# Denominators and gating logits of three pairs in one bank, normalized behind the transposes

## The chip, the cores and the metric

The kernel runs on one core of one Trainium2 chip. The metric is the device time of one execution in microseconds (us). A core has TensorE (PE in the profile, its weight loads PEld), VectorE (DVE), ScalarE (ACT), GpSimd (POOL) and SyncE (SP); each takes its instructions in a fixed order and waits for others by semaphores. PE writes its results into PSUM, in banks of 512 fp32 columns by 128 partitions. SP and POOL also start DMA transfers, each from a queue of its own.

## What is computed

Attention with a soft cap on the scores, over 8 batches, 12 heads, 448 tokens and a head size of 64, followed by a mixture of experts with one expert out of 8 per token:

```python
scores = cap * np.tanh(scale * np.matmul(q, k.transpose(0, 1, 3, 2)) / cap)
attn = np.exp(scores - np.max(scores, axis=-1, keepdims=True))
attn = attn / (np.sum(attn, axis=-1, keepdims=True) + 1e-09)
x = np.matmul(attn, v)                     # -> (3584, 768), a token's 12 heads side by side
logits = x @ w_gate + modality_bias[modality_id]
e_idx = np.argmax(logits, axis=1)
# gate_w: the softmax of the logits at e_idx
out[mask] = gate_w[mask, None] * (np.maximum(x[mask] @ w1[e], 0.0) @ w2[e])   # mask = e_idx == e
```

## The kernel before

**Attention.** The work goes by pairs of heads: 6 pairs a batch, 48 in all, numbered g. For a pair, `kq` holds keys and queries of both heads (head j in the 64 partitions from 64 j). `prep(g + 1)` loads the next pair: `kq` and `va` (the values) by SP, `hi` (a rounded copy of `kq`, which POOL's queue loads with a conversion) and `lo`, the remainder, on DVE (line 432). `scores` has four steps: three of 128 own keys of each head, and one in which the last 64 keys of both heads share the 128 partitions. Each step makes products hi x hi, lo x hi, hi x lo on PE (line 443), then tanh and exp on ACT (lines 445, 446) into `pt`, transposed: keys on partitions, queries along the columns. Two score tiles are in PSUM in turn.

The weighted values of pair g − 1 are made during pair g: `weigh_own` between the second and third score step, `weigh_shared` behind the fourth; `xT` has the two heads' dimensions on the partitions and queries along columns. `add_up` sums `pt` over the key blocks on DVE into `tot`. A pair later (g − 2 during pair g) `normalize` multiplies `tot` by a matrix of ones on PE, which gives the denominators `den` already spread over the 64 partitions of their head; DVE takes the reciprocal of this 128 x 448 tile (line 463) and multiplies (line 465, `xn`). `rows_out` transposes `xn` to rows of tokens (line 482, four transposes), and DVE copies them into `xs` (line 484). Behind every third pair `gate` makes the gating logits of the three pairs, in three groups of 32 columns of one bank `glog` (line 491), summed over the two triples of a batch, and POOL starts the store of `xs` to `xd` in DRAM.

**Routing.** Behind a batch's last pair `logits` transposes `glog` to tokens (lines 498 to 502), and `route` finds on DVE the expert of each token, its weight, and by two small matmuls (`rank`, lines 232 and 233) its place among that expert's tokens; an iota (line 247) and four indirect DMAs (line 256) on POOL write token number and weight into the map `mapd`. After seven batches `early_slot` chooses the expert of a first slot of 384 tokens, whose map (`rows`), tokens (`gather`, by indirect DMA on POOL) and first-layer weights (`load_raw`, `split_w`) are fetched while the last pairs run; `MOVES` puts the transposes of the gathered tokens. After the last batch `slots` plans all other slots on DVE.

**Experts.** Per slot `ffn1` (8 blocks of 128 columns, 18 matmuls each) and `ffn2` (six half-outputs of 24 matmuls); `ahead` fetches the next slot's map rows and tokens, which `ffn2` transposes between its half-outputs.

**Order.** What passes through `pin` keeps the program's order on its engine; this is so for nearly all of PE's attention work and for SP's loads. All other instructions are ordered engine by engine when the kernel is built, by a planner that takes what is ready first by its own estimate of times. So the order on DVE, ACT and POOL is fixed before the run, and an instruction that waits holds all that stand behind it on its engine.

## Time and profile before

| | |
|---|---|
| median of 3 runs | 1071.52 us (1067.74 to 1072.17) |
| profiled execution | 1074.64 us, span 1073.1 us |
| busy: PE / DVE / ACT / POOL | 935.8 / 693.0 / 566.2 / 148.8 us |
| mean granted TensorE clock | 0.938 |
| first expert matmul | 543.0 us from the start of the span |

The profile gives the busy time of each engine, the groups of instructions with their mean duration in ns, what an engine waited for in the idle time before an instruction (in square brackets or behind "<-", with the line of the releasing instruction), and in a stretch of time the TensorE clock that the throttle granted, as a share of full speed. A busy PE is not PE at its peak, since matmuls are pipelined; differences between the starts of instructions that follow without a pause say what a block of them costs.

### The profile page before, as it was taken

Reading aid. Unit: us, or ns where it says so; the run is one execution under the profiler, and the core shown is the slowest. Engines: PE = TensorE matmul, PEld = TensorE weight load, DVE = VectorE, ACT = ScalarE, POOL = GpSimd, SP = SyncE. Lnnn points to the kernel's source line nnn. Section 1 sums busy time; section 2 is a strip of 40 time slices with the busy share of each in tenths; the row PEclk is TensorE's granted clock in tenths of the full one; section 3 lists DMA queues with packets and bytes.
Section 4 is the critical chain, followed back from the end, with each engine's and each line's share of the span. In section 5 each row is a group of like instructions: output and inputs, shape, how many; then the busy total and the mean of one; then the engine's idle time right before and its main releaser. Section 6 shows DMA issues by size and latency. Waiting matters only on the chain. (4 is left out here: it accounts for less than half of the span.)

```text
span 1073.1 us, 14468 instructions
## 1 busy us (share of the span) xinstructions
PE 935.8 (87%) x5232; PEld 713.9 (67%) x5232; DVE 693.0 (65%) x978; ACT 566.2 (53%) x759; POOL 148.8 (14%) x191
## 2 busy tenths in 40 slices
PE   7786878689787786874789999999999999999996
PEld 3343444344343443432359999999999999998896
DVE  5897888969798787884975443434444444447762
ACT  7675667667575675654614444434443434345551
POOL 2002020010202002021013202020201011101100
PEclk9898889989898898887889999999999999999997
DMA  5454435525354354446417646453636463535760
GB/s 152 140 159 134 141 120 162 166 79 166 119 166 138 94 165 124 146 121 164 146 37 237 217 131 211 150 193 132 206 118 206 133 191 133 177 135 197 246 202 10
DMA packets 53803, 162.62 MB, mean 152 GB/s; under 512 B 9422, under 2 KB 9934, under 8 KB 53712
## 3 DMA queue, kind: packets, MB, share of 16 engines
q1 hardware_dynamic: 38000, 105.78, 31.1%
q0 software_dynamic: 15568, 55.72, 16.6%
q8 instruction: 46, 0.75, 0.3%
q14 instruction: 45, 0.37, 0.1%
q10 hardware_dynamic: 144, 0.00, 0.0%
HBM read 139.96 MB, written 22.69 MB: 152 GB/s over the span
## 5 line engine op out<-in xcount | busy, mean ns | idle before, releaser
L445 ACT ACTIVATE th<-sc,isc 128x896 f32<-128x896 f32 x192 | 169.5, 909 | 139.6 <-PE sc L443 135.2
L446 ACT ACTIVATE pt<-th,cabs 128x896 f32<-128x896 f32 x192 | 176.8, 949 | 2.9
L689 PE MATMUL ph<-x,al 128*128 128x384 f32 (+2 forms) x528 | 168.0, 318 | 0.0
L711 PE MATMUL py<-bh,hh 128*128 128x384 f32 x464 | 158.4, 342 | 2.7 <-ACT bh L641 2.7
L463 DVE RECIPROCAL rec<-den 128x448 f32<-128x448 f32 x48 | 141.7, 2953 | 27.0 <-PE den L461 26.5
L711 PE MATMUL py<-bh,hl 128*128 128x384 f32 x464 | 155.7, 336 | 0.0
L711 PE MATMUL py<-bl,hh 128*128 128x384 f32 x464 | 155.2, 334 | 0.0
L685 PE MATMUL ph<-x,ah 128*128 128x384 f32 x384 | 129.3, 337 | 1.6 <-DVE plan L383 1.5
L686 PE MATMUL ph<-x,ah 128*128 128x384 f32 x384 | 129.3, 337 | 0.0
L642 DVE TENSOR_TENSOR bl<-raw,bh 128x768 fp32r<-128x768 f32 x88 | 82.1, 955 | 68.3 <-ACT bh L641 62.3
L472 PE MATMUL xT<-pt,va 128*64 128x448 f32 x576 | 121.0, 556 | 0.0
L641 ACT CAST bh<-raw 128x768 fp32r<-128x768 f32 x88 | 71.7, 840 | 70.4 <-DMA raw<-in_w_dram 60.1
L689 PEld LDWEIGHTS ph<-x,al 128*128 128x128 f32 x528 | 102.1, 193 | 0.7 <-issue 0.7
L642 DVE TENSOR_TENSOR al<-raw,ah 128x1024 fp32r<-128x1024 f32 x66 | 79.6, 1223 | 31.6 <-ACT ah L641 31.2
L472 PEld LDWEIGHTS xT<-pt,va 128*64 128x64 f32 x576 | 43.8, 147 | 78.2 <-issue 71.2
L443 PE MATMUL sc<-hi 64*128 64x448 f32 (+1 forms) x336 | 93.2, 484 | 2.9 <-ACT th L445 2.3
L482 PE MATMUL tp<-ident,xn 128*112 128x128 f32 x192 | 31.2, 287 | 73.4 <-DVE xn L465 68.2
L482 PEld LDWEIGHTS tp<-ident,xn 128*112 128x112 f32 x192 | 21.0, 138 | 102.7 <-issue 77.9
L711 PEld LDWEIGHTS py<-bh,hh 128*128 128x128 f32 x464 | 87.0, 188 | 3.1 <-ACT bh L641 3.0
L721 POOL DMA_INDIRECT out_dram<-ot,mt x29 | 33.1, 1141 | 396.3 <-ACT ot L716 319.5
L711 PEld LDWEIGHTS py<-bh,hl 128*128 128x128 f32 x464 | 87.1, 188 | 0.2 <-DVE hl L696 0.2
L711 PEld LDWEIGHTS py<-bl,hh 128*128 128x128 f32 x464 | 87.2, 188 | 0.0
(155 smaller groups left out, 1424.2 us busy)
## 6 DMA issues: line engine op xcount, KB each, us to landing
raw<-in_w_dram SPq DMA_DIRECT2D x66, 512.0 KB, 4.4
raw<-in_w_dram SPq DMA_DIRECT2D x88, 384.0 KB, 4.0
kq<-in_kq_dram SPq DMA_DIRECT2D x47, 480.0 KB, 3.4
hi<-in_kq_dram POOLq DMA_DIRECT2D x46, 480.0 KB, 6.9
va<-in_v_dram SPq DMA_DIRECT2D x48, 256.0 KB, 4.1
xd<-xs POOLq DMA_DIRECT2D x16, 672.0 KB, 4.4
mapd<-pay,pos POOLq DMA_INDIRECT x32, 3.3
xg<-xd,mt POOLq DMA_INDIRECT x30, 6.0
```

The source lines that it names most:

```text
L443: pin(pe.matmul(sc[:, j, :S], k[rows, ks], q[rows, KC2:], start=i == 0, stop=i == 2))
L445: nc.scalar.activation(th[:, :n], sc[:, :n, :S], AF.Tanh, scale=self.isc)
L446: nc.scalar.activation(pt[:, 2 * step : 2 * step + n], th[:, :n], AF.Exp, scale=self.cabs)
L463: nc.vector.reciprocal(rec, den[:, :S])
L472: pin(pe.matmul(xT[j * D : (j + 1) * D, :S], va[:, u * D : (u + 1) * D], pt[:, u], start=i == 0, stop=False))
L482: pin(pe.transpose(tp[:CP, c * 128 : (c + 1) * 128], xn[:, c * CP : (c + 1) * CP], self.ident))
L641: a = self.nc.scalar.copy(hi, raw)
L642: b = self.nc.vector.tensor_tensor(lo, raw, hi, op=ALU.subtract)
L685: nc.tensor.matmul(ph[:, :w], hi[:, fs], self.x[:, k, 0, :w], start=first, stop=False)
L686: nc.tensor.matmul(ph[:, :w], hi[:, fs], self.x[:, k, 1, :w], start=False, stop=False)
L689: nc.tensor.matmul(ph[:, :w], lo[:, fs], self.x[:, k, 0, :w], start=False, stop=last)
L711: nc.tensor.matmul(py[:, :HALF], self.h[a][:, f, rows], self.w2s[f][c][:, cs], start=i == 0, stop=i == 3 * FC - 1,)
```

## The change

- The denominators are no longer spread over 64 partitions. `sums` collects for three pairs at a time, in one bank with 32 columns per pair, four parts: the column sums of `tot` of head 0 and of head 1, those of the shared keys `sh`, each by a weight matrix `pick` with ones in column 16 or 17, and the gating logits of both heads from the values that aren't normalized (columns 0 to 15). They stand behind `weigh_own`: parts 0 and 1 in the second pair of the next triple, parts 2 and 3 in its third.
- `by_token` transposes this bank for each triple; `logits` takes the reciprocals of 24 columns per partition and multiplies the logits. `rows_out` transposes the `xT` that isn't normalized, copied from PSUM to SBUF pairs before, and multiplies by the reciprocals as it leaves PSUM. The three pairs of a triple are transposed together, one pair behind the logits.
- The exp of the shared keys goes to a tile `sh` of its own; `add_up`'s two half adds go.
- `route` is cut in two: the part up to the counts behind the logits, `rank` and the writing of the map behind the next pair's `weigh_own`; both `rank` matmuls and the count are pinned. For the last batch the second part stands behind the second block of the first `ffn1`, and `slots` behind the fourth; the fetch for the next slot then comes behind this `ffn1`.
- The early slot's map is read one pair later, its gather two pairs later; four first-layer weight blocks are loaded at once behind pair 45, with four staging buffers instead of three.
- One PSUM bank for `xT` instead of two, one more for the transposes.

```diff
-NU = 2 * KU + 1
 OWN = KU * 128
 KC2 = OWN + 2 * KR
 QK = KC2 + S
+GE = 2 * E
...
+        self.pick = cpool.tile([128, 3, GW], F32, name="pick")
+        nc.vector.memset(self.pick, 0.0)
+        for j in range(2):
+            nc.vector.memset(self.pick[:, j, GE + j : GE + j + 1], 1.0)
+            nc.vector.memset(self.pick[j * KR : (j + 1) * KR, 2, GE + j : GE + j + 1], 1.0)
...
         nc.vector.tensor_tensor(self.acc, before[:, C - 1], oh[:, C - 1], op=ALU.add)
+        yield
         rank = ps.tile([128, 512], F32, name="rank", tag="small")
         rk = rank[:CP, : C * E]
-        nc.tensor.matmul(rk, self.tri, oh.rearrange("p c e -> p (c e)"), start=True, stop=False)
-        nc.tensor.matmul(rk, self.ones[:, :CP], before.rearrange("p c e -> p (c e)"), start=False, stop=True)
+        self.pin(nc.tensor.matmul(rk, self.tri, oh.rearrange("p c e -> p (c e)"), start=True, stop=False))
+        self.pin(
+            nc.tensor.matmul(rk, self.ones[:, :CP], before.rearrange("p c e -> p (c e)"), start=False, stop=True)
+        )
...
-        nc.tensor.matmul(cps[:, :E], self.ones[:, :128], self.acc, start=True, stop=True)
+        self.pin(nc.tensor.matmul(cps[:, :E], self.ones[:, :128], self.acc, start=True, stop=True))
...
-            xp = st.enter_context(tc.tile_pool(name="xp", bufs=2))
-            rp = st.enter_context(tc.tile_pool(name="rp", bufs=1))
+            xp = st.enter_context(tc.tile_pool(name="xp", bufs=1))
             ps_s = st.enter_context(tc.tile_pool(name="ps_s", bufs=2, space=PSUM))
-            ps_x = st.enter_context(tc.tile_pool(name="ps_x", bufs=2, space=PSUM))
+            ps_x = st.enter_context(tc.tile_pool(name="ps_x", bufs=1, space=PSUM))
             ps_g = st.enter_context(tc.tile_pool(name="ps_g", bufs=1, space=PSUM))
+            ps_v = st.enter_context(tc.tile_pool(name="ps_v", bufs=1, space=PSUM))
...
+                dst = pt[:, 2 * step : 2 * step + 2] if step < KU else sh
+                nc.scalar.activation(dst, th[:, :n] if step < KU else th[:, 0], AF.Exp, scale=self.cabs)
 
             def weigh_own(xT, pt, va):
...
+                for u in range(2 * KU):
+                    j = u % 2
+                    pin(pe.matmul(
+                        xT[j * D : (j + 1) * D, :S], va[:, u * D : (u + 1) * D], pt[:, u], start=u < 2, stop=False
+                    ))
+
+            def weigh_shared(xT, sh, va):
+                pin(pe.matmul(xT[:, :S], va[:, 2 * KU * D :], sh, start=False, stop=True))
+
+            def sums(h, part):
+
+                if part == 0:
                     self.glog = ps_g.tile([128, 512], F32, name="glog")
...
+                for t in range(HB):
+                    xs_, tot, sh = kept[h * HB + t]
+                    w = self.pick[:, part] if part < 3 else self.wgt[:, (h * HB + t) % NP]
+                    rhs = (tot[:, 0], tot[:, 1], sh, xs_)[part]
+                    pin(pe.matmul(self.glog[t * GW : (t + 1) * GW, :S], w, rhs, start=part == 0, stop=part == 3))
+
+            def by_token():
+
+                w = HB * GW
+                gl = xp.tile([w, S], F32, name="gl")
+                nc.vector.tensor_copy(gl, self.glog[:w, :S])
                 lt = self.ps_r.tile([128, 512], F32, name="lt", tag="small")
-                w = HB * GW
                 for c in range(C):
                     pin(pe.transpose(lt[:CP, c * w : (c + 1) * w], gl[:, c * CP : (c + 1) * CP], self.ident[:w, :w]))
-                return lt[:CP, : C * w].rearrange("p (c t x) -> p c x t", c=C, t=HB)[:, :, :E]
+                return lt[:CP, : C * w].rearrange("p (c t x) -> p c t x", c=C, t=HB)
+
+            def logits(h, lt, lg):
+                rec = xp.tile([CP, C, HB, 2], F32, name="rec", bufs=2)
+                nc.vector.reciprocal(rec, lt[:, :, :, GE : GE + 2])
+                h0 = h % NH * 2 * HB
+                for j in range(2):
+                    nc.vector.tensor_tensor(
+                        lg[:, :, h0 + j : h0 + 2 * HB : 2], lt[:, :, :, j * E : (j + 1) * E],
+                        rec[:, :, :, j : j + 1].to_broadcast([CP, C, HB, E]), op=ALU.mult,
+                    )
+                return rec
+
+            def rows_out(h, t, xs, rec):
+                xT = kept.pop(h * HB + t)[0]
+                pool, tag = (self.ps_r, "small") if t == 1 else (ps_v, "tp")
+                tp = pool.tile([128, 512], F32, name="tp", tag=tag)
+                for c in range(C):
+                    pin(pe.transpose(tp[:CP, c * 128 : (c + 1) * 128], xT[:, c * CP : (c + 1) * CP], self.ident))
+                nc.vector.tensor_tensor(
+                    xs[:, :, t * 128 : (t + 1) * 128].rearrange("p c (j d) -> p c j d", j=2),
+                    tp[:CP].rearrange("p (c j d) -> p c j d", c=C, j=2),
+                    rec[:, :, t].unsqueeze(3).to_broadcast([CP, C, 2, D]),
+                    op=ALU.mult,
+                )
+
+            def store(h, xs):
+                b, h0 = divmod(h, NH)
+                nc.gpsimd.dma_start(
+                    self.xd[b * S : (b + 1) * S, h0 * HB * 128 : (h0 + 1) * HB * 128].rearrange("(p c) f -> p c f", c=C),
+                    xs,
+                )
...
             SPLITS = {
...
+                (NG - 2, 1): (0,),
+                (NG - 2, 3): (1,),
+                (NG - 1, 1): (2,),
+                (NG - 1, 3): (3,),
+                (NG - 0, 0): (4,),
+                (NG - 0, 1): (5,),
             }
-            MOVES = {(NG - 1, 3): (0, 1), (NG, 0): (2, 3), (NG, 1): (4, 5)}
+            MOVES = {(NG - 1, 3): (0, 1), (NG, 1): (2, 3), (NG, 3): (4, 5)}
...
+            for g in range(NG + 1):
                 if g < NG:
-                    pt = pp.tile([128, NU, S], F32, name="pt")
+                    pt = pp.tile([128, 2 * KU, S], F32, name="pt")
+                    sh = xp.tile([128, S], F32, name="sh", bufs=HB + 2)
                     cur = ready
                 for step in range(C):
                     if step % 2 == 0 and g < NG:
-                        scores(step, pt, *cur[:2])
-                        scores(step + 1, pt, *cur[:2])
+                        scores(step, pt, sh, *cur[:2])
+                        scores(step + 1, pt, sh, *cur[:2])
                     if step == 1:
                         if g + 1 < NG:
                             ready = prep(g + 1)
...
+                        if g:
+                            ppt, psh, pva = pend
+                            tot = xp.tile([128, 2, S], F32, name="tot", bufs=HB + 1)
+                            nc.vector.tensor_tensor(tot, ppt[:, 0:2], ppt[:, 2:4], op=ALU.add)
+                            nc.vector.tensor_tensor(tot, tot, ppt[:, 4:6], op=ALU.add)
                             xT = ps_x.tile([128, 512], F32, name="xT")
                             weigh_own(xT, ppt, pva)
+
+                        if g > HB:
+                            h, r = divmod(g - HB - 1, HB)
+                            if r < 2:
+                                sums(h, 2 * r)
+                                sums(h, 2 * r + 1)
+                        if g in routing:
+                            next(routing[g], None)
+                            del routing[g]
                     if step == 3:
                         if g == 3:
                             self.empty_map()
                         if g == 2:
                             self.gate_bias()
...
+                        if g:
+                            weigh_shared(xT, psh, pva)
+                            xs_ = xp.tile([128, S], F32, name="xT", bufs=HB + 3)
+                            nc.vector.tensor_copy(xs_, xT[:, :S])
+                            kept[g - 1] = xs_, tot, psh
+                        if g > HB:
+                            h, r = divmod(g - HB - 1, HB)
+                            b = h // NH
+                            if r == 1:
+                                if h % NH == 0:
+                                    lgs[b] = xp.tile([CP, C, H, E], F32, name="lg")
+                                lt = by_token()
+                                rec = logits(h, lt, lgs[b])
+                                if h % NH == NH - 1:
+                                    way = self.route(b, lgs[b], rp, self.ps_r)
+                                    next(way)
+                                    routing[g + 1] = way
+                            if r == 2:
                                 xs = xp.tile([CP, C, HB * 128], F32, name="xs")
...
+                                for t in range(HB):
+                                    rows_out(h, t, xs, rec)
+                                store(h, xs)
+                                if h == NH * (B - 1) - 1:
                                     meta = self.early_slot(self.cpool, self.ps_r)
                     for k in SPLITS.get((g, step), ()):
                         self.split_w(raws[k], self.w1s[k], pin=True)
+                        if len(raws) < KC:
+                            raws.append(self.load_raw(e, self.w1, len(raws), FF))
                     for k in MOVES.get((g, step), ()):
                         self.transpose(k, (ps_s, self.ps_r)[k % 2], ("sc", "small")[k % 2], busy=k < 2)
                 if g < NG:
...
+                    pend = pt, sh, cur[2]
+                if g == NG - 3:
                     e = self.expert(meta, 0)
                     early = e, self.rows(meta, 0)
+                    raws = [self.load_raw(e, self.w1, k, FF) for k in range(self.nstage)]
+                if g == NG - 2:
                     self.gather(early[1], known=NT - S)
-                    raws = [self.load_raw(e, self.w1, k, FF) for k in range(2)]
-            return early
+            self.raws = [self.load_raw(e, self.w2, k, DM) for k in range(self.nstage)]
+            h = NG // HB - 1
+            for part in range(4):
+                sums(h, part)
+            rec = logits(h, by_token(), lgs[B - 1])
+            way = self.route(B - 1, lgs[B - 1], rp, self.ps_r)
+            next(way)
+            xs = xp.tile([CP, C, HB * 128], F32, name="xs")
+            for t in range(HB):
+                rows_out(h, t, xs, rec)
+            store(h, xs)
+            return early, way
...
+            for at, work in between:
+                if at == f:
+                    work()
...
-        nxt = ahead() if ahead else None
-        self.ffn1(n)
+        nxt = ahead() if ahead and not between else None
+        self.ffn1(n, between)
+        if between:
...
-            self.nstage = 3
+            self.nstage = 4
...
-                        early = self.attention(qk, first)
                         rt = sb.enter_context(tc.tile_pool(name="rt", bufs=1))
-                        meta = self.slots(rt, self.ps_r, True)
+                        early, way = self.attention(qk, first, rt)
                         self.moe_pools2(sb)
-                        self.run_slots(early, meta)
+
+                        def order():
+                            self.meta = self.slots(rt, self.ps_r, True)
+
+                        self.run_slots(early, ((1, lambda: next(way, None)), (3, order)))
...
-    wgb = np.zeros((128, NP, GW), wg.dtype)
-    wgb[:, :, :E] = wg.reshape(NP, 128, E).swapaxes(0, 1)
+    wgb = np.zeros((2, D, NP, GW), wg.dtype)
+    for j in range(2):
+        wgb[j, :, :, j * E : (j + 1) * E] = wg.reshape(NP, 2, D, E)[:, j].swapaxes(0, 1)
...
```

More of the change, by code (lines that the diff above doesn't have):

```diff
@@ L72 @@
 HB = 3
+NH = NP // HB
 class Program:
@@ L403, in load_kq, with attention @@
         return kq
-    def attention(self, qk, first):
+    def attention(self, qk, first, rp):
         tc, nc = self.tc, self.nc
@@ L445, in scores @@
                 nc.scalar.activation(th[:, :n], sc[:, :n, :S], AF.Tanh, scale=self.isc)
-                nc.scalar.activation(pt[:, 2 * step : 2 * step + n], th[:, :n], AF.Exp, scale=self.cabs)
-            def add_up(pt):
-                tot = pp.tile([128, 2, S], F32, name="tot")
-                nc.vector.tensor_tensor(tot, pt[:, 0:2], pt[:, 2:4], op=ALU.add)
-                nc.vector.tensor_tensor(tot, tot, pt[:, 4:6], op=ALU.add)
-                for j in range(2):
-                    rows = slice(j * KR, (j + 1) * KR)
-                    nc.vector.tensor_tensor(tot[rows, j], tot[rows, j], pt[rows, 2 * KU], op=ALU.add)
-                return tot
@@ L458, in normalize @@
-            def normalize(xT, tot):
-                den = self.ps_r.tile([128, 512], F32, name="den", tag="small")
-                for j in range(2):
-                    pin(pe.matmul(den[j * D : (j + 1) * D, :S], self.ones1, tot[:, j], start=True, stop=True))
-                rec = rp.tile([128, S], F32, name="rec")
-                nc.vector.reciprocal(rec, den[:, :S])
-                xn = xp.tile([128, S], F32, name="xn", bufs=HB + 1)
-                nc.vector.tensor_tensor(xn, xT[:, :S], rec, op=ALU.mult)
-                return xn
@@ L486, in gate @@
-            def gate(h0, xns):
-                if h0 == 0:
-                    self.glog = ps_g.tile([128, 512], F32, name="glog")
-                for t, xn in enumerate(xns):
-                    pin(pe.matmul(
-                        self.glog[t * GW : (t + 1) * GW, :S], self.wgt[:, h0 * HB + t], xn,
-                        start=h0 == 0, stop=h0 == NP // HB - 1,
-                    ))
-            def logits():
-                gl = rp.tile([HB * GW, S], F32, name="gl")
-                nc.vector.tensor_copy(gl, self.glog[: HB * GW, :S])
+                dst = pt[:, 2 * step : 2 * step + 2] if step < KU else sh
@@ L518, in attention @@
             self.gate_weights()
-            early, xns, state = None, [], {}
-            for g in range(NG + 2):
+            kept, lgs, routing, raws = {}, {}, {}, []
+            for g in range(NG + 1):
                 if g < NG:
-                    pt = pp.tile([128, NU, S], F32, name="pt")
+                    pt = pp.tile([128, 2 * KU, S], F32, name="pt")
+                    sh = xp.tile([128, S], F32, name="sh", bufs=HB + 2)
                     cur = ready
@@ L724, in ffn2, with run_slot @@
             )
-    def run_slot(self, cur, n, ahead=None, raws=()):
+    def run_slot(self, cur, n, ahead=None, raws=(), between=()):
         moves = []
@@ L743, in run_slot, with run_slots @@
         return nxt
-    def run_slots(self, cur, meta):
+    def run_slots(self, cur, order):
         tc, nc = self.tc, self.nc
@@ L749, in ahead @@
         def ahead(i, n=TW):
+            meta = self.meta
             if i == 0:
@@ L760, in run_slots @@
                 which = nc.values_load(self.plani[0:1, 2:3], min_val=0, max_val=len(ENDS))
-            cur = self.run_slot(cur, TW, lambda: ahead(i), self.raws if i == 0 else ())
+            cur = self.run_slot(cur, TW, lambda: ahead(i), *((self.raws, order) if i == 0 else ()))
         self.finish(which, len(ENDS) - 1, cur, ahead)
```

75 lines of the change are left out of this document (11 added, 64 removed).

## The prediction

> **What bounds the kernel now.** I read the page, then busy time by stage, then TensorE's rows in order of time, then the waits. The stages:
>
> ```profile
> span 1073.1 us, 14468 instructions
> ```
>
> ```profile
> 38.00:476.00 438.00, 350.65 (x1877) 176.19 (x1874) 371.11 (x468) 287.25 (x334) 56.00 (x85) 0.91 0.45 139
> 476.00:561.50 85.50, 59.80 (x296) 33.51 (x295) 61.01 (x127) 38.73 (x49) 13.39 (x17) 0.80 0.41 110
> 561.50:1064.00 502.50, 498.12 (x2938) 490.65 (x2938) 237.75 (x353) 216.61 (x348) 71.78 (x67) 0.99 0.52 172
> 147.28:210.73 63.45, 51.04 (x276) 25.89 (x277) 54.02 (x69) 42.35 (x49) 8.64 (x13) 0.92 0.46 140
> ```
>
> Columns: stretch, length, busy time and count of PE, PEld, DVE, ACT, POOL, then granted clock, DMA share, GB/s. From 561.5 on PE is busy 498 of 502 us: the experts are PE's, and this change leaves their matmuls alone. In the attention no engine is full: PE 80%, DVE 85%, ACT 66%, at a clock of 0.91. The last row is one batch (six pairs): 63.45 us, of which PE works 51. So a chain bounds it. One pair, on PE:
>
> ```profile
> 179.79 0.92 PE L477 MATMUL xT<-pt,va 128*128 128x448 f32 x2
> 180.54 0.62 PE L482 MATMUL tp<-ident,xn 128*112 128x128 f32 x4
> 181.09 0.95 PE L491 MATMUL glog<-xn,wgt 128*32 128x448 f32 x6
> 181.98 0.47 PE L443 MATMUL sc<-hi 64*128 64x448 f32 x2
> ```
>
> ```profile
> 183.39 0.97 PE L461 MATMUL den<-tot,ones 128*64 128x448 f32 x4
> 184.19 2.42 PE L472 MATMUL xT<-pt,va 128*64 128x448 f32 x12
> 186.55 0.47 PE L443 MATMUL sc<-hi 64*128 64x448 f32 x2
> ```
>
> ```profile
> 188.08 0.91 PE L477 MATMUL xT<-pt,va 128*128 128x448 f32 x2
> 190.67 0.62 PE L482 MATMUL tp<-ident,xn 128*112 128x128 f32 x4 [1.68 <-DVE xn L465]
> 191.22 0.47 PE L443 MATMUL sc<-hi 64*128 64x448 f32 x2
> ```
>
> Differences of starts give PE's price at full clock: first two score steps 1.41, den 0.80, own keys 2.36, last two score steps 1.53, shared keys 0.75 (179.79 to 180.54), four transposes 0.55, three gate matmuls 0.89. The pair lasts 9.24 us, and 1.68 of it PE stands before the transposes, which need xn: they wait for den, then the reciprocal, then the multiply on DVE. Over the run, and what DVE pays (mean ns behind the busy time):
>
> ```profile
> PE tp L482 <- DVE xn L465: 68.2, 28, 14.5
> ```
>
> ```profile
> L463 DVE RECIPROCAL rec<-den 128x448 f32<-128x448 f32 x48 | 141.7, 2953 | 27.0 <-PE den L461 26.5
> L455 DVE TENSOR_TENSOR tot<-tot,pt 64x448 f32<-64x448 f32 x96 | 59.1, 616 | 5.0
> L432 DVE TENSOR_TENSOR lo<-kq,hi 128x960 fp32r<-128x960 f32 x47 | 54.0, 1148 | 44.6 <-DMA hi<-in_kq_dram 44.6
> L484 DVE COPY xs<-tp 112x512 f32<-112x512 f32 x48 | 33.0, 687 | 14.9 <-PE tp L482 14.6
> L465 DVE TENSOR_TENSOR xn<-xT,rec 128x448 f32<-128x448 f32 x48 | 29.7, 619 | 0.9
> L498 DVE COPY gl<-glog 96x448 f32<-96x448 f32 x8 | 4.9, 614 | 0.2 <-PE glog L491 0.2
> ```
>
> The routing at the end of each batch:
>
> ```profile
> 210.73 0.55 PE L502 MATMUL lt<-ident,gl 96*112 96x96 f32 x4 [1.53 <-DVE gl L498]
> 214.35 0.28 PE L232 MATMUL rank<-oh,tri 112*112 112x32 bf16 x1 [3.08 <-DVE oh L223]
> ```
>
> ```profile
> 215.05 0.74 PE L443 MATMUL sc<-hi 64*128 64x448 f32 x2
> ```
>
> ```profile
> 221.86 0.47 PE L443 MATMUL sc<-hi 64*128 64x448 f32 x2
> ```
>
> PE stands 4.6 us here, and then the work of 4.57 us (1.41 + 0.80 + 2.36) takes 6.81: a pause of this length costs 2.2 us of clock besides itself. Two pairs later the same routing strikes again, through POOL's queue:
>
> ```profile
> 216.86 1.00 POOL L256 DMA_INDIRECT mapd<-pay,pos  x1 [6.71 <-DVE pos L243]
> ```
>
> ```profile
> 225.31 0.13 POOL L247 IOTA pay<- 112x4 int32 x1 [3.68 <-DMA mapd<-pay,pos]
> 225.84 0.58 POOL L428 DMA_DIRECT2D hi<-in_kq_dram  x1 [0.41 <-PE sc L443]
> ```
>
> ```profile
> 231.14 1.16 DVE L432 TENSOR_TENSOR lo<-kq,hi 128x960 fp32r<-128x960 f32 x1 [3.97 <-DMA hi<-in_kq_dram]
> ```
>
> ```profile
> 236.62 0.79 PE L482 MATMUL tp<-ident,xn 128*112 128x128 f32 x4 [4.95 <-DVE xn L465]
> ```
>
> Four scatters and an iota that waits for their landing hold the load of hi; DVE stands in lo; the reciprocal is queued behind lo, and xn behind that.
>
> **The change, part by part.** *PE.* Den (0.80 a pair) goes. Each triple of pairs gets four parts of sums of three matmuls with 32 columns, the shape of the gate row, so 0.89 each. The logits' transposes (0.55) come twice a batch. Before: 6 x (1.41 + 0.80 + 2.36 + 1.53 + 0.75 + 0.55) = 44.4, gate 1.8, lt 0.55, rank 0.6: 47.4 us a batch. After: 6 x (1.41 + 2.36 + 1.53 + 0.75) = 36.3, sums 8 x 0.89 = 7.1, lt 1.1, transposes 3.3, rank 0.6: 48.4. PE gets 1 us more to do; nothing is saved there.
>
> *DVE.* Per pair the reciprocal (2.95), two half adds (1.23), the xn multiply (0.62) and the copy xs (0.69) go; a copy of xT (0.62, by xn's row) and a multiply in the place of the copy (0.69, by its shape; 0.6 to 1.4, the upper end if the broadcast operand halved the rate) come. Per triple come gl (0.61, once a batch until now), a reciprocal of 24 elements (24/448 of 2953 plus a start: 0.3 by estimate) and two multiplies of 96 (0.3 each by estimate). From 54.0 us a batch DVE falls by 6 x 4.18 and rises by some 2.4: about 31. That itself frees no time; what frees it is that the transposes read an xT finished pairs ago.
>
> *ACT* keeps its work, 42.35 us a batch (7.06 a pair): below PE's 48.4, so not the bound.
>
> *Waits that go,* in that batch: 63.45 − 47.4 = 16 us of pauses and low clock. *Waits that come or stay,* per batch, none shown by this trace as such:
> - the lt transposes behind gl, twice: 0 to 1.53 (the lt row), and now two score steps and the shared matmuls lie between, 2.3 us against a copy of 0.61; I take 0.7 each;
> - rank is pinned behind the next pair's own keys, 3.8 us after lt; the chain lt to rank took 3.6, and gets a reciprocal, two multiplies and perhaps two sums ahead of it: 0 to 3, I take 2. Behind it stand the last two score steps, and ACT behind these;
> - the third transposes of a triple reuse the first's bank, behind a multiply of 0.69 while the second's 0.55 run: 0.2 to 0.7, I take 0.5, twice;
> - one xT bank instead of two: own keys wait for the xT copy, with 1.41 of scores for 0.62 of copy: 0 to 2, I take 1;
> - the scatters (5 us of POOL) are issued a pair later, still ahead of a load of hi. This load then has PE's pair and a half to land in; 0 (covered) to 4.95 + 2.2 (as at 236.62); I take 1, nearer to cover, because no reciprocal stands between lo and PE any more.
> Sum 6.4: **54.8 us a batch, 9.13 a pair**; no pause above 3 us, so full clock.
>
> *The end of the attention.*
>
> ```profile
> 44.16 0.47 PE L443 MATMUL sc<-hi 64*128 64x448 f32 x2
> ```
>
> ```profile
> 506.39 1.16 DVE L432 TENSOR_TENSOR lo<-kq,hi 128x960 fp32r<-128x960 f32 x1 [13.53 <-DMA hi<-in_kq_dram]
> ```
>
> ```profile
> 508.23 1.07 PE L482 MATMUL tp<-ident,xn 128*112 128x128 f32 x4 [14.53 <-DVE xn L465]
> ```
>
> ```profile
> 528.10 0.45 PE L661 MATMUL ptr<-identr,xg 128*128 128x128 f32 x3
> ```
>
> ```profile
> 535.84 1.76 PE L461 MATMUL den<-tot,ones 128*64 128x448 f32 x4 [1.16 <-DVE x L671]
> ```
>
> ```profile
> 543.02 0.45 PE L685 MATMUL ph<-x,ah 128*128 128x384 f32 x1
> ```
>
> ```profile
> 556.40 0.34 PE L689 MATMUL ph<-x,al 128*128 128x384 f32 x1
> ```
>
> ```profile
> 561.54 0.69 PE L685 MATMUL ph<-x,ah 128*128 128x384 f32 x1 [1.51 <-DVE plan L383]
> ```
>
> Pairs 4 to 47 took 44.16 to 528.10 = 484 us, with one pause of 14.5: the early slot's map read and gather went ahead of two loads of hi on POOL. The change reads the map one pair later and gathers two later, behind the last hi; instead four W1 loads of 512 KB go into SP's queue in one go ahead of the last pair's kq and va. Four at the 4.4 us to landing that the page gives for one are up to 17 us ahead of a kq that has a pair to land: 0 to 14.5, I take 8, and 2 for the splits that are moved into the last pairs. After: 44 x 9.13 + 10 = 412. Gain 72.
>
> Pairs 0 to 3 (to 44.16) have neither den nor transposes any more (0.80 + 0.55 each): gain 5.
>
> From 528.10 to 561.54, 33.4 us, 54 matmuls of the first expert ran (9.2 us at 498.12/2938); 24 us are the attention's rest. After: own and shared keys 3.1, six times four transposes 3.3, sums 3.6, lt 0.55, expert transposes 1.5, with 5 of waits: 17. Gain 7. The second half of the last routing and the plan of the slots move between the first expert's matmuls, which cover them (25 us of PE). What is late next is the gather for the second slot, issued some 15 us after the plan and wanted two half-outputs into the second layer: 0 to 5, I take 2.
>
> Sum: 1073.1 − 72 − 5 − 7 + 2 = **991**. The profiled run took 1074.64 us, 1.5 above its span; the median of the runs shown, 1071.52, is 3.1 under it. These two nearly cancel, so I stay with 991.
>
> **A rule against it.** In a triple's last pair twelve transposes now stand together, about 2.2 to 3 us with the wait. The row at 535.84 follows three bursts of transposes with pauses of 1 to 2.4 us and shows den at 1.76 against 0.97, the slow clock; pauses or transposes could be the cause. The Trainium skill, TensorE: Matmul & The Clock Gate, Part 4 (PE-mode transpose), says that transposes do not keep the clock up as other matmuls do. By that rule each triple would lose the clock once; this trace neither proves nor excludes it.
>
> **The rivals.**
> 1. *The waits move to hi and stay.* The order of POOL's queue again puts the iota before a load of hi, lo stands on DVE, and now xT's copy, gl and the multiplies are queued behind it. For: lo waited 44.6 us for hi in this trace. Against: PE's need for DVE is now a pair old or more. Price 4.95 + 0.8 of clock in each of 7 batches: +40, **1031**.
> 2. *Everything is covered.* A batch of 50 us, 8.33 a pair: 44 x 0.8 = 35 less, **956**. For: DVE at 31 of 50 us is free when called. Against: ACT at 42.35 of 50 leaves little slack.
> 3. *Transposes drop the clock:* 16 triples x 2.2 = +35, **1026**.
> 4. *Slower: rank behind lo.* Rank is pinned within the scores. If DVE's order has the lo after next ahead of the routing chain and that hi is held by the scatters or the store of xs, PE stands for both. It decides from 82/7 = 12 us a batch; one such wait of 13.53 stands at 506.39, none of the others reaches 6. At 13.5 in 7 batches: +94, **1085**.
> 5. *Nothing is gained:* ACT or the loads of hi set 11 us a pair already. Against: pairs of 8.5 to 9.24 occur. About 1071.
>
> **How the numbers follow.** Forecast 991 (own range 973 to 1011) 0.5; rival 1 0.2; rival 2 0.15; rival 3 0.07; rival 4 0.05; rival 5 0.03. The range from 953 to 1035 takes in 1, 2 and 3 at their prices, leaving out 4, 5 and the edges of the others. Half a per cent (5 us) is about what a measurement tells from no change: faster 0.92, same 0.03, slower 0.05.
>
> **What would show it.** Right: a pair near 9 us between score starts, PE over 88% busy before the experts at a clock of 0.97 or more, no wait of tp for xn's successor, DVE near 31 us a batch, rank waits under 3 us. Wrong: pauses of 4 us or more once a batch before scores or rank, with a late hi on POOL; a low clock behind each twelve transposes; a wait of the last pair's scores for kq beyond 10 us.

## The result, and the profile after

| | before | after |
|---|---|---|
| median of 4 runs | 1069.99 us (1067.74 to 1072.17) | 1010.3 us (1007.03 to 1013.86) |
| span of the profiled execution | 1073.1 us | 1008.5 us |

The ratio is 0.9443 (95% interval 0.9403 to 0.9483), 60 us less; forecast was 991, with a range of 953 to 1035.

Busy time by stage after the change, in the columns of before (the second row is one batch):

```profile
span 1008.5 us, 14612 instructions
...
38.00:438.73 400.73, 358.30 (x2088) 179.94 (x2084) 228.58 (x412) 294.48 (x350) 70.43 (x91) 0.96 0.56 157
189.82:246.94 57.12, 51.37 (x294) 25.76 (x293) 32.15 (x57) 41.38 (x50) 10.19 (x14) 0.94 0.60 156
438.73:472.26 33.53, 21.54 (x120) 10.16 (x120) 20.16 (x28) 16.75 (x22) 4.39 (x5) 0.78 0.58 206
472.26:1000.00 527.74, 514.10 (x3016) 503.75 (x3013) 248.00 (x418) 218.00 (x355) 75.20 (x72) 0.98 0.50 165
```

PE is now busy for 89% of the attention's loop, at a clock of 0.96. In a batch it works as long as before (51.4 against 51.0 us, low clock included), and the batch is 6.3 us shorter. DVE fell from 54.02 to 32.15. The second logit transposes of the first and of the seventh batch:

```profile
77.70 0.50 PE L484 MATMUL lt<-ident,gl 96*112 96x96 f32 x4
...
414.10 0.50 PE L484 MATMUL lt<-ident,gl 96*112 96x96 f32 x4
```

Six batches lie between: 56.07 us each. PE around the routing, in order of time (start, length):

```profile
139.99 0.22 PE L238 MATMUL rank<-oh,tri 112*112 112x32 bf16 x1 [1.66 <-DVE oh L228]
140.58 0.18 PE L240 MATMUL rank<-before,ones 112*112 112x32 bf16 x1 [0.36 <-DVE before L233]
140.68 0.47 PE L451 MATMUL sc<-hi 64*128 64x448 f32 x2
...
142.97 1.04 PE L503 MATMUL tp<-ident,xT 128*112 128x128 f32 x8
144.45 0.65 PE L503 MATMUL tp<-ident,xT 128*112 128x128 f32 x4 [0.44 <-DVE xs L504]
145.03 0.47 PE L451 MATMUL sc<-hi 64*128 64x448 f32 x2
...
146.44 2.48 PE L460 MATMUL xT<-pt,va 128*64 128x448 f32 x12
148.85 1.70 PE L475 MATMUL glog<-tot,pick 128*32 128x448 f32 x12
150.48 0.47 PE L451 MATMUL sc<-hi 64*128 64x448 f32 x2
...
155.61 0.48 PE L451 MATMUL sc<-hi 64*128 64x448 f32 x2 [2.69 <-DMA hi<-in_kq_dram]
156.71 0.74 PE L451 MATMUL sc<-hi,lo 64*128 64x448 f32 x2 [0.62 <-DVE lo L440]
...
158.87 2.99 PE L460 MATMUL xT<-pt,va 128*64 128x448 f32 x12
161.79 0.95 PE L475 MATMUL glog<-sh,pick 128*32 128x448 f32 x6
```

No transpose waits for `xn` or anything in its place any more. These waits were 68.2 us in all; what is left is the third transposes of a triple, which reuse a bank (sum, count and longest, us):

```profile
PE tp L503 <- DVE xs L504: 7.0, 14, 1.1
```

The largest pause of the batch stands before the scores at 155.61, whose `hi` and `lo` are late, and behind it the same matmuls run slower: 0.74 against 0.47, 2.99 against 2.48. The reason is on POOL's queue and then on DVE:

```profile
143.24 1.00 POOL L264 DMA_INDIRECT mapd<-pay,pos  x1 [8.99 <-DVE pos L251]
...
149.34 0.60 POOL L436 DMA_DIRECT2D hi<-in_kq_dram  x1
...
155.50 1.16 DVE L440 TENSOR_TENSOR lo<-kq,hi 128x960 fp32r<-128x960 f32 x1 [8.91 <-DMA hi<-in_kq_dram]
```

The four writes of the map keep the load of `hi` from being issued until 149.34, although its buffer came free at 142.4 (the end of the score matmuls that start at 142.02). Over the run the scores' waits for `hi` sum to 12.9 us in six batches, 1.21 to 3.15 us each.

### The profile page after: what moved, and what is told of

Read it like the earlier page. It is cut to its first block, busy times and chain, and to the rows that moved or that the text cites. A ratio compares the mean times of both kernels' runs of the same rounds, so it can differ in the third digit from the quotient of the medians.

```text
span 1008.5 us, 14612 instructions
## 1 busy us (share of the span) xinstructions
PE 926.6 (92%) x5360; PEld 709.5 (70%) x5360; DVE 516.7 (51%) x894; ACT 557.2 (55%) x759; POOL 157.9 (16%) x191
## 5 line engine op out<-in xcount | busy, mean ns | idle before, releaser
L455 ACT ACTIVATE pt<-th,cabs 128x896 f32<-128x896 f32 x144 | 148.0, 1042 | 2.0
L460 PE MATMUL xT<-pt,va 128*64 128x448 f32 x576 | 127.8, 582 | 1.9 <-DVE xT L569 1.9
L440 DVE TENSOR_TENSOR lo<-kq,hi 128x960 fp32r<-128x960 f32 (+2 forms) x49 | 55.6, 1137 | 105.6 <-DMA hi<-in_kq_dram 83.8
L451 PE MATMUL sc<-hi 64*128 64x448 f32 (+1 forms) x336 | 88.4, 453 | 21.5 <-DMA hi<-in_kq_dram 12.9
L451 PEld LDWEIGHTS sc<-hi 64*128 64x128 f32 (+1 forms) x336 | 37.2, 190 | 88.6 <-issue 31.6
L753 ACT ACTIVATE ot<-py,mt 128x384 f32<-128x384 f32 x58 | 33.6, 580 | 98.4 <-PE py L748 53.9
L460 PEld LDWEIGHTS xT<-pt,va 128*64 128x64 f32 x576 | 39.5, 146 | 68.7 <-issue 54.2
```

The source lines that it names most:

```text
L440: keep(nc.vector.tensor_tensor(lo[:, cs], kq[:, cs], hi[:, cs], op=ALU.subtract))
L451: pin(pe.matmul(sc[:, j, :S], k[rows, ks], q[rows, KC2:], start=i == 0, stop=i == 2))
L455: nc.scalar.activation(dst, th[:, :n] if step < KU else th[:, 0], AF.Exp, scale=self.cabs)
L460: pin(pe.matmul(xT[j * D : (j + 1) * D, :S], va[:, u * D : (u + 1) * D], pt[:, u], start=u < 2, stop=False))
L753: nc.scalar.mul(ot[:, cs], py[:, :HALF], mt[:, t, 1:2])
```

## Where the gain comes from

Theory: the transposes' new distance makes the gain, the order on POOL takes some of it back, and DVE's lighter load is a by-product. Rivals: the gain is DVE's load; the gain is the spread-out routing. All runs stand against a kernel before on their own chip, so ratios are compared.

**The routing in one piece.** In the loop both halves of `route` stand behind the logits again.

```diff
-                                    way = self.route(b, lgs[b], rp, self.ps_r)
-                                    next(way)
-                                    routing[g + 1] = way
+                                    for _ in self.route(b, lgs[b], rp, self.ps_r):
+                                        pass
```

> The changed kernel with routing in one piece again: inside the loop rank follows the logits at once, nothing else is undone. Theory (the gain is that transposes and scores no longer wait for a chain den, reciprocal, multiply; spreading the routing matters little): rank stands 3.5 to 5 us behind lt in place of 2.0 and the clock may drop once a batch (2.2 us), but the scatters start some 4 us earlier, so the load of hi behind them is late by less than the 3.3 us of now. Net -3 to +4 us a batch: 990 to 1038 us, most likely 1015. Rival (the spread of the routing is the gain): the 4.6 us pause and 2.2 us of clock of the kernel before come back in each of 7 batches, +48: about 1058 us.

Measured: 1013.75 us, ratio 0.9436 (0.9403 to 0.947), the same as with the routing spread out, as the theory had it. Its waits and their sums, counts and maxima:

```profile
PE rank L238 <- DVE oh L228: 33.2, 6, 5.9
```

`rank` now costs up to 5.9 us in a batch (1.8 in the changed kernel), but the scores' waits for `hi`, 12.9 us in all in the changed kernel, are 0.3 here: one pause replaces the other.

**The kernel before, with its routing split.** The other side of this; the choice of the early slot, which needs the counts, moves a pair back with it, and the last batch's routing stays in one piece:

```diff
+        yield
         rank = ps.tile([128, 512], F32, name="rank", tag="small")
...
+                                next(way)
+                                routing[g + 1] = way
```

> The kernel before, with the routing alone cut in two pieces a pair apart; its denominators and logits stay as they were, a reciprocal of 128x448 twice a pair and the transposes behind it. Theory (spreading the routing is worth little by itself): 1060-1075. Rival (the routing's chain was the wait that counted before too): 1030-1050.

Measured: 1069.26 us, ratio 0.9971 (0.9944 to 0.9998): 3 us of the 60, as the theory had it. (The expectation's "twice a pair" is a slip: the reciprocal stands there once a pair.)

```profile
PE tp L483 <- DVE xn L466: 76.9, 35, 9.2
PE rank L233 <- DVE acc L229: 11.4, 7, 2.0
```

The waits for `rank` fell from 21.7 us (18.5 and 3.2 by their two releasers) to 11.4; those of the transposes for `xn` rose from 68.2 to 76.9.

**DVE loaded again.** To each pair of the changed kernel comes a reciprocal of 128x448 that nobody reads, behind `tot`.

```diff
                             nc.vector.tensor_tensor(tot, tot, ppt[:, 4:6], op=ALU.add)
+                            junk = xp.tile([128, S], F32, name="junk")
+                            nc.vector.reciprocal(junk, tot[:, 0])
```

> The changed kernel with a reciprocal of 128x448 per pair whose result nobody reads, on DVE behind the sums of tot. Theory (the chain was the cost, not DVE's load): DVE rises from 32 to about 50 us a batch of 56, and only what is queued behind it (lo, xT's copy, the routing chain before rank) comes later: 0 to 3 us a batch, 1010 to 1034 us, with the gain over the kernel before kept by more than half. Rival (DVE's load was the bound): with DVE back at 50 us the period goes back toward 63 us a batch, 1050 us or more.

Measured: 1065.44 us, ratio 0.9932 (0.9899 to 0.9965); its ten runs spread from 1058.87 to 1073.95, and the profile is of the shortest. Nearly all the gain is gone, with the transposes as far behind as in the changed kernel. The theory falls in this point. What PE waits for:

```profile
PE rank L238 <- DVE oh L228: 44.8, 6, 8.4
PE xT L460 <- DVE xT L571: 14.0, 8, 2.6
```

The routing's chain and the copies of `xT` stand behind the block in DVE's order. The transposes' waits did not come back: 8.2 us, against 7.0 in the changed kernel. So the new distance does take away that one wait, but with a loaded DVE PE stands at `rank` instead (52.1 us with the last batch's 7.3, against 10.9), and a batch takes 62.4 us.

**Load, or the place of the block?** The same reciprocal only in the one pair of a batch whose DVE queue carries the routing's chain (`if g in routing`), and only in the others (`if g not in routing`):

```diff
+                            if g in routing:          # the other kernel: if g not in routing
+                                junk = xp.tile([128, S], F32, name="junk")
+                                nc.vector.reciprocal(junk, tot[:, 0])
```

> An unread reciprocal of 128x448 on DVE only in the one pair of each batch whose queue carries the routing's chain, 2.95 us a batch, 21 us in all. If the loss with one in every pair (1010 to 1065) came from the block that stands in DVE's fixed order ahead of the routing's chain, whose rank matmul PE meets in order: 4-7 us a batch are lost here too, 1040-1060 us. If it came from the load on DVE as such (six blocks a batch), a sixth of the loss: 1015-1022.

> The same unread reciprocal in the other five pairs of each batch and not in the one with the routing's chain: 14.8 us more on DVE a batch, 46.9 of some 56. By the block ahead of the routing's chain: at most the waits for the copies of xT (1.5 to 2.6 us once a batch), 1012-1030 us. By the load on DVE: five sixths of the loss, 1050-1060.

Measured: 1031.67 us, ratio 0.9622 (0.956 to 0.9685), and 1039.34 us, ratio 0.9695 (0.964 to 0.975). Neither theory got its numbers. Against the changed kernel's 0.9443 and at 1070 us for 1, seven blocks ahead of the routing cost some 19 us, 2.7 each (1.6 to 3.9 by the intervals) at a length of 2.95; the 41 others cost 27, 0.7 each (0.5 to 0.8); with all 48 it was 52. The first one's waits, and its DVE in the second batch:

```profile
PE rank L238 <- DVE oh L228: 31.3, 6, 5.6
```

```profile
143.20 2.94 DVE L552 RECIPROCAL junk<-tot 128x448 f32<-128x448 f32 x1
```

So a block in the routing's chain costs about four times one elsewhere. It stands within the chain, and an add of `tot` (1.07 us) that followed the chain in the changed kernel now stands within it too: `rank` waits 5.40 us in this batch where it waited 1.66, and the next scores take 0.74 instead of 0.47. In return the waits for `hi` fall from 12.9 to 4.1 us, so that 2.7 is what is left of several effects, and that it is near the block's length is chance. With the other blocks the routing is late too (25.9 us in all, 10.9 in the changed kernel): the `lo` that stands in the middle of the chain waits 2.95 us for its `hi` in the second batch, where it waited 0.29, and `rank` waits 4.26. Even with all the blocks DVE worked only 315.43 of the 400 us from 38 to 438, and still PE stood.

## Where the gain stopped: the pause that moves

**The map writes behind the next `hi`: three tries.** In the first, the writes were to go a pair later, and loads of `hi` were pinned.

```diff
+        yield
         puts = []
...
+            self.pin(put)
...
-                    nc.gpsimd.dma_start(hi, self.kq[b, hp])
+                    pin(nc.gpsimd.dma_start(hi, self.kq[b, hp]))
```

> The changed kernel with the four map scatters of batches 0 to 5 one pair later, behind the next load of hi on POOL (both kept in program order). Theory (the load of hi waits behind four scatters, so once a batch the scores wait 2.7 us for hi and 0.6 for lo, and the clock drops): 6 times 3.3 + about 2 us: 978 to 992 us, and no wait of the scores for hi over 1 us in batches 0 to 5. Rival (hi is late by DMA traffic or by its own landing of 4.4 us, not by the queue): 1003 to 1010 us.

Measured: 1061.02 us, ratio 0.9899 (0.9864 to 0.9935). The edit changed another order than meant: the map writes stayed ahead, and the token numbers and the store came before the load as well. POOL and PE:

```profile
161.55 0.13 POOL L255 IOTA pay<- 112x4 int32 x1 [4.32 <-DMA mapd<-pay,pos]
162.15 0.72 POOL L515 DMA_DIRECT2D xd<-xs  x1 [0.48 <-issue]
162.81 1.21 POOL L438 DMA_DIRECT2D hi<-in_kq_dram  x2
```

```profile
170.00 0.74 PE L453 MATMUL sc<-hi 64*128 64x448 f32 x2 [6.64 <-DMA hi<-in_kq_dram]
```

This is the first rival of the prediction, built by mistake: with the iota, which waits for the landing of the writes, ahead of `hi`, the scores' waits for `hi` grow from 12.9 to 55.8 us, and 49 of the 60 us are lost. In the second try the writes were tied behind the load last traced, by an edge in the program:

```diff
+            with self.tc.issue_after(self.last_hi.ins):
                 put = nc.gpsimd.indirect_dma_start(
```

> The four map writes of a batch are held on POOL's queue behind the load of the next pair's hi; nothing else is changed. In the profile after the change the load stood behind them once a batch (map writes from 143.24 to 149.34, load issued 149.34), the scores waited 2.69 us for hi and 0.62 for lo, and the following scores and weights ran at the low clock (2.99 against 2.48 us for the twelve weights), some 5 us a batch in all. Theory (the wait that is left once a batch is POOL's order): hi is there in time, a batch falls from 56.1 to 51-52 us, the time from 1010 to 975-985 us. Rival (the load is late because the DMA queues are busy, or another wait stands right behind, the lo or the tanh of ScalarE): 1000-1015.

Measured: 1012.51 us, ratio 0.9432 (0.9368 to 0.9496). This load stood ahead of the writes already; the late one is of the pair after. The order is the old one, and so is the time. The third try also moves the writes a pair later (the `yield` of the first try) and ties them behind the load that had followed them, for all batches but the last two.

> The earlier edit held the map writes behind a load of hi that stood ahead of them anyhow: POOL's order was the old one, and its time says nothing of that order. Here the four map writes of a batch are issued a pair later, tied behind the load of hi that had followed them (all batches but the last two, whose map rows are read soon). The order on POOL becomes three loads of hi, four map writes, the xd store, the token numbers, three loads. Theory (what is left once a batch is POOL's order): no 2.7-3.1 us wait for hi and no low clock after it in six batches, some 5 us each: 975-985 us. Rival 1 (the store of xd and the token numbers, now ahead of the next hi, make that one late instead): 1000-1015. Rival 2 (the clock falls at the next pause, that for the rank, so that only the wait itself comes back, 3 us a batch): 990-996.

Measured: 1011.88 us, ratio 0.942 (0.9382 to 0.9458), although the order is now the one wanted. POOL, then DVE, then PE, in the second batch:

```profile
144.42 0.53 POOL L438 DMA_DIRECT2D hi<-in_kq_dram  x1 [8.59 <-PE sc L455]
145.32 1.00 POOL L266 DMA_INDIRECT mapd<-pay,pos  x1 [0.38 <-issue]
...
158.22 0.13 POOL L255 IOTA pay<- 112x4 int32 x1 [6.00 <-DMA mapd<-pay,pos]
158.76 0.59 POOL L438 DMA_DIRECT2D hi<-in_kq_dram  x1 [0.42 <-issue]
```

```profile
162.76 1.16 DVE L444 TENSOR_TENSOR lo<-kq,hi 128x960 fp32r<-128x960 f32 x1 [6.01 <-DMA hi<-in_kq_dram]
...
164.83 0.61 DVE L485 COPY gl<-glog 96x448 f32<-96x448 f32 x1
```

```profile
165.50 0.89 PE L488 MATMUL lt<-ident,gl 96*112 96x96 f32 x4 [3.02 <-DVE gl L485]
```

The scores' wait is gone, and in its place the transposes of the logits wait, 22.2 us in six batches, with the low clock behind them again. The iota writes the tile that the four writes read and waits for their landing; the next `hi` is behind the iota, `lo` behind this `hi`, and `gl`, which has nothing to do with it, behind `lo` in DVE's order. That is its rival 1, with `gl` as the place. A wait that is bound to POOL's order was moved by one load, not removed.

**The first-layer weights behind the last pair's loads.** The first four W1 loads, which stood ahead of the last `kq` and `va` on SP's queue, go behind them; three of the four splits follow a step later.

```diff
-                    raws = [self.load_raw(e, self.w1, k, FF) for k in range(self.nstage)]
...
+                        if g == NG - 2:
+                            raws = [self.load_raw(e, self.w1, k, FF) for k in range(self.nstage)]
```

> The changed kernel with the four first-layer weight loads issued behind the last pair's kq and va instead of ahead of them, and the splits of these weights one step later each. Theory (the two pauses of 7.3 and 6.7 us at 433 to 447 us of the changed kernel come from the weight loads that go ahead of kq on SP, and from the split that stands on ACT before a tanh): both go, with about 3 us of low clock: 990 to 998 us. Rival (the load of hi behind the scatters holds this pair as it holds one pair of each batch): only the ACT part goes, 1003 to 1008 us.

Measured: 1010.27 us, ratio 0.9421 (0.9379 to 0.9463): no gain, outside both expectations. Two pauses at the end of the attention became one:

```profile
444.88 0.74 PE L451 MATMUL sc<-hi 64*128 64x448 f32 x2 [6.43 <-DMA hi<-in_kq_dram]
```

From the seventh batch's logit transposes to the last pair's it is 36.5 us instead of 43.8, so the edit wins 7.3 us at its place. But PE's waits for `hi` sum to 21.6 us in this run (6.43 of them here), and the seventh batch ended 5.7 us later, though the edit leaves these batches alone; why they ran longer isn't shown. A batch took 56.7 us in this profile and 56.8 in that of the run below with the plan ahead, so some 4 us between two profiles can come from six equal batches. The same edit with the second try (and a second buffer for the map rows):

> The same, with two more edits: the first expert's six W1 loads behind the last pair's kq and v (as in the earlier run of that edit alone), and two buffers for the map rows, so that the token numbers' write does not wait for the last map write. Theory: with hi ahead of the map writes the last pair's load no longer waits 6.4 us, and the pauses at the end of attention fall from 14 us and a low clock to some 4: 960-975 us, 8-14 under the run with hi first alone. Rival (the W1 loads only move the pause to the first expert's splits): within 4 us of hi first alone.

Measured: 1007.05 us, ratio 0.9385 (0.9333 to 0.9437); with the third try:

> The same with the first expert's W1 loads behind the last pair's kq and v, and two buffers for the map rows. Theory: 4-8 us under the run with the map writes alone, 968-980 us; the last pair's hi still stands behind map writes there, as in the earlier run, so that a pause of some 6 us stays at the end. Rival: the two edits together gain nothing over the first, 980-996.

Measured: 1011.78 us, ratio 0.94 (0.9348 to 0.9453). Neither stands apart from the changed kernel, and both expectations of the last run, which start from a gain of the third try, were missed. The second buffer didn't free the iota (it waited 7.05 us in the second batch): as many iotas as there are buffers are placed at the program's start, and the next one then waits for the batch just written.

**The plan ahead of the first expert.** The last batch's rank, map writes and plan of slots go back to where they were.

```diff
-                        self.run_slots(early, ((1, lambda: next(way, None)), (3, order)))
+                        next(way, None)
+                        self.meta = self.slots(rt, self.ps_r, True)
+                        self.run_slots(early, ())
```

> The last batch's rank, map writes and the plan of slots stand again ahead of the first expert's layer, where they were before the change; all else as in the changed kernel. By the prediction's term (7 us gained by the move, 2 given back by the late gather): 1015 us, +5. Rival (the gather that comes late in the expert phase costs what the move gains): 1007-1012. Rival 2 (PE stands for the whole chain of rank, plan and table): 1020-1030.

Measured: 1008.56 us, ratio 0.9396 (0.936 to 0.9431). The move gains nothing that these times show, as the first rival said. Busy time by stretches of the changed kernel, then of this one:

```profile
500.00:520.00 20.00, 17.98 (x102) 17.19 (x100) 10.85 (x37) 7.07 (x9) 8.35 (x13) 1.00 0.70 219
520.00:540.00 20.00, 18.44 (x105) 18.22 (x106) 7.86 (x11) 8.57 (x15) 8.26 (x8) 0.91 0.56 182
```

```profile
500.00:520.00 20.00, 20.00 (x117) 20.00 (x116) 9.48 (x12) 8.01 (x13) 7.75 (x10) 1.00 0.61 208
520.00:540.00 20.00, 20.00 (x126) 19.89 (x125) 8.89 (x12) 9.72 (x17) 6.13 (x5) 1.00 0.50 160
```

The table's write is issued at 491.31 instead of 503.79, the gathers are in time, and from 500 to 540 PE doesn't stand. But ahead of that it stands in the first expert for its second-layer weights and its hidden rows:

```profile
490.16 0.61 PE L748 MATMUL py<-bh,hh 128*128 128x384 f32 x2 [1.55 <-ACT bh L672]
492.29 0.62 PE L748 MATMUL py<-bl,hh 128*128 128x384 f32 x2 [1.51 <-DVE bl L673]
495.37 0.69 PE L719 MATMUL ph<-x,ah 128*128 128x384 f32 x1 [2.46 <-DVE hl L730]
```

PE meets the rank matmuls among the expert's here too (482.64), so that the early plan holds nothing up on PE itself; the times of the two kernels can't be told apart. By the two profiles, from the first expert matmul to the end it is 529.6 us with the plan ahead and 536.2 without, so some 7 us in the experts seem to hang on the late plan; the longer batches of this run (4.8 us more to the seventh's end) hide most of it in the sum.

## Why the prediction was right or wrong

The stretches of the profiled executions, against its terms:

| stretch | forecast | measured |
|---|---|---|
| to pair 4's first scores | −5 | 44.16 to 37.26: −6.9 |
| pairs 4 to 47 | −72 | 484 to 420.6 (37.26 to 457.86): −63.3 |
| the rest | −7 + 2 | 545.0 to 550.6: +5.6 |

**Right: the direction, and nearly what a batch takes.** A batch takes 56.07 us where 54.8 were forecast. In the batch shown, `rank` waits 1.66 + 0.36 (taken as 2) and the third transposes 0.44 (0.5); DVE works 32 us a batch (31), and the new small operations cost what was estimated:

```profile
L504 DVE TENSOR_TENSOR xs<-tp,rec 112x512 f32<-112x512 f32 x48 | 31.7, 682 | 2.1 <-DMA xd<-xs 1.0 <-PE tp L503 0.8
L492 DVE TENSOR_TENSOR lg<-lt,rec 112x96 f32<-112x96 f32 x32 | 6.7, 252 | 0.5
L489 DVE RECIPROCAL rec<-lt 112x24 f32<-112x24 f32 x16 | 4.8, 298 | 0.8 <-PE lt L484 0.8
```

The broadcast operand of the multiply cost nothing (682 ns against 687 for the copy in its place before). The two parts of the sums take 1.63 (148.85 to 150.48) where 2 x 0.89 were counted.

**Mis-sized: the load of `hi` behind the scatters.** It was taken as 1 a batch, "nearer to cover", of 0 to 7.15. In the batch shown, the second, it costs 2.69 + 0.62 of waits, and the scores and weights from 155.61 to 161.79 take 0.62 of these and 1.7 more than at full speed (1.41 and 2.41): 5.0. Over six batches the wait for `hi` averages 2.15. The reason given for cover, that no reciprocal stands between `lo` and PE, looked at the wrong consumer: the scores themselves read `hi`. The logits' transposes (2 x 0.7 taken) didn't wait, and own keys waited for the copy of `xT` only 1.9 us in the whole run (1 a batch taken), and over six batches all pauses together come to 5.5 us a batch (56.07 less 50.5 of work), under the 6.4 of the forecast. Rival 1's price for this wait, 4.95 + 0.8 a batch, was nearer (its 0.8 of clock is too small for its own row: behind 236.62 in the kernel before, transposes, scores and `den` take some 1.5 us more than at full clock), though here the scatters alone do it; with the iota ahead of the load as well, as rival 1 had it, a run gave 1061.

**Wrong: "no pause above 3 us, so full clock".** From 77.70 to 414.10 PE works 50.5 us a batch at a clock of 0.95 where 48.4 were counted at full clock. These 2.1 us are more than the 1.3 by which the batch missed. Pauses under 3 us were enough: in the first batch `rank` waits 1.54 and 0.30 (83.56 and 84.06), and at 85.00 the scores take 0.74, where they take 0.48 at the same point (141.49) behind the 1.66 of the second batch.

```profile
85.00 0.74 PE L451 MATMUL sc<-hi 128*128 128x448 f32 x1
```

**Wrong: "That itself frees no time"** of DVE's fall. A single unread reciprocal per pair, 17.7 of the 22 us a batch that DVE lost, takes back some 52 of 60 us. What the new distance of the transposes saved is kept only while DVE has nothing long ahead of the routing's chain, `lo` and the copy of `xT`. The sum came out since the batch was priced from PE's work and small waits, which presume a free DVE. So the mechanism named for the gain was half of it: the distance takes away the transposes' wait, and the lighter DVE keeps that wait from coming back at `rank`. How much the distance of the transposes gives by itself isn't settled: no run has it with all of the old DVE work in the old order.

**Wrong: the end.** The seven gained ahead of the experts are there (14.4 us from 457.86 to the first expert matmul at 472.26, and some 3 of transposes and rank among the experts', 17 forecast), but some 12 are lost in the experts where the late gather was taken as 2. Its rows:

```profile
486.84 0.45 PE L748 MATMUL py<-bh,hh 128*128 128x384 f32 x1 [2.08 <-ACT hh L729]
...
520.40 0.28 PE L692 MATMUL ptr<-identr,xg 128*128 128x128 f32 x1 [1.49 <-DMA xg<-xd,mt]
```

The waits for gathered tokens sum to 3.1 us. Pauses in the first expert and the low clock behind them (0.88 from 480 to 490, 0.91 from 520 to 540) are the likely rest; it isn't added up here. The run with the plan ahead, 6.6 us shorter in the experts, speaks for the late plan as half of the 12. The wait for the last pair's loads, taken as 8 and 2, is two pauses:

```profile
440.01 0.74 PE L451 MATMUL sc<-hi 64*128 64x448 f32 x2 [7.27 <-ACT th L453]
...
447.48 0.74 PE L451 MATMUL sc<-hi,lo 64*128 64x448 f32 x2 [6.73 <-DVE lo L440]
```

14.0 us; but pairs 4 to 6 start 7.9 to 8.2 us apart (37.26, 45.14, 53.30), so that what lies beyond 44 pairs of 9.345 is 9.4, the 10 of the sum by chance.

**Not borne out: the transposes and the clock.** Behind the twelve transposes at 142.97 and 144.45 the scores at 145.03 take 1.41 us to the own keys at 146.44, full speed; the two score matmuls behind the transposes take 0.47 at all 14 such places of the loop. The Trainium skill, TensorE: Matmul & The Clock Gate, Part 4 (PE-mode transpose), says that the full clock doesn't engage for transposes; twelve of them, 2 us with their wait, didn't let it fall here. Where the transposes themselves ran slowly (2.50 us at 311.83), the clock had fallen before them, behind a wait for `rank`. Nothing here speaks for rival 3. Rival 4 (rank behind `lo`) exists as a mechanism: `rank` is late by a `lo` in its chain, but by 2 us and not 13.5.

## What to carry to other kernels

On an engine with a fixed order the place of an instruction counts more than the busy share: 2.95 us in a chain that the bounding engine awaits cost about 2.7, elsewhere 0.7, on an engine that was idle for a fifth of the time or more. When a pause is bound to a queue (POOL's writes, the iota, the load), moving one instruction hands it to the next consumer (from `hi` to `gl`, or from `hi` to `rank`) at about the same price, 1010 to 1014 us each time; follow the queue to the instruction that waits for a landing, here the iota. An iota with a tile of its own for each batch should take that wait away; that wasn't tried.

## What the runs showed of the hardware

- In the changed kernel the low clock followed pauses of very different length, and not always: behind 2.69 us before the scores, with 0.62 behind it (0.74 for the next two matmuls), but also behind 1.54 and 0.30 before `rank` (0.74 at 85.00) and behind 1.34 for `hi` and 0.64 for `lo` at 99.25 (4.17 instead of 2.48 for the next twelve weights); not behind 1.66 before `rank` at 139.99. In the run with the writes a pair later it followed 3.02 before `lt` at once. The length of one pause doesn't decide it here.
- The iota's wait for the landing of the four map writes was 2.90 us in the second batch of the changed kernel, 6.00 and 7.05 us with the writes a pair later.
- In the run with the W1 loads of 512 KB behind the last `kq`, the scores got the last pair's `hi` some 10 us after its issue (434.75 to 444.88), where the changed kernel's page gives 4.4 from issue to landing as the median of all 46.
